# Seven small unread transfers that shift which DMA engines carry the 8-row loads of a sparse-attention and spectral-mixing kernel

## The chip, the cores and the metric

The kernel runs on one core of a Trainium2 chip. The metric is the time of one execution on the device, in microseconds, from the first to the last instruction of that core. Before the change the median of three runs is 434.43 us (434.22, 434.43 and 436.14).

A core has five engines that work side by side, each with its own stream of instructions: TensorE (PE in the profile; its weight loads are PEld), VectorE (DVE), ScalarE (ACT), GpSimd (POOL) and SyncE (SP). Data come from the chip's memory to on-chip memory by 16 DMA engines, which the five engines give work to.

## The reference

The program is an attention with two kinds of sparse masks, followed by a mixing of frequencies and a channel product:

```python
# q, k, v: (8, 8, 576, 64) float32
scores = scale * q @ k^T
mask: heads 0-3: 0 <= i - j < 32          # local
      heads 4-7: j <= i and i % 32 == j % 32   # strided
attn = softmax(scores where mask else -1e9) @ v
x = attn as (8, 576, 512)
X = rfft(x over the 576 positions)             # the first 64 modes are kept
Y[m] = X[m] @ (w_r[m] + 1j * w_i[m])           # 512 x 512 per mode
y = irfft(Y)
u = x + y
out = u + max(u @ w_ch, 0)                     # float32
```

The 64 pairs of matrices w_r and w_i are 134 MB in float32, by far the largest input. Each is used once for 8 batch entries. q, k and v together are 28 MB.

## The kernel before, in words

The batch has 8 entries, called images here. The kernel goes through four stages.

1. Strided heads of all images (the loop around line 746). For each image, 72 rows of 2048 numbers are loaded for each of v, q and k: 4 heads by 18 blocks of 32 positions. They are turned by TensorE, scored, masked, exponentiated and multiplied with v.
2. Local heads of all images (the loop around line 775), with the products of the first half of the modes' weights between them.
3. The second half of the weights (the loop around line 846), with the turning of x and the first parts of the channel product between them.
4. A tail (from line 859) with the last modes, the inverse transform as a matrix product and the output.

The weights are the stream that runs through all of it. `w_fetch` (L174) loads the weights of two modes: one transfer for w_r (L196) and one for w_i, each of 64 rows of 2 x 2048 numbers, which are cast from float32 to float16 on the way. Nearly all loads, those of the weights, of q, k and v, are issued by GpSimd, and therefore stand in one order, the order of the program. The order is written out by hand (`manual_schedule`).

The loads of the strided rows are made by `load_str` (L219). For images 0 and 1 there is one transfer of 64 rows for each tensor and image (L229); later a transfer of 64 rows takes two images at once (L227). The remaining 8 of the 72 rows are always loaded for two images at once, by L231, right behind the 64-row load of the even image. So there are twelve 8-row loads in all: for v, q and k of the image pairs 0/1, 2/3, 4/5 and 6/7. They go into `ring`, a buffer of 12 slots that the local heads' rows (`load_loc`, L233) use later.

The order of the calls matters for the change: `load_str(0)`, `load_str(1)`, `load_str(2)` and one `w_fetch` come ahead of the loop. In the loop, image 1 has `load_str(4)` behind the weights fetched at image 0, and image 3 has `load_str(6)`; behind each come further calls of `w_fetch` and, from image 4 on, the loads of the local rows.

Each transfer that GpSimd issues counts up one of eight semaphores in turn. An issue waits until the transfer eight places before it has landed, and for whatever its buffer needs: that TensorE has read what stood in the slot, for instance.

`pat` (L155) is the pool of buffers that the attention stages use. Its buffers exist once each (bufs=1). A second buffer that is asked for under the same name is the same memory, and whoever writes it waits for the earlier use to end.

Of the kernel before, what the change touches and what calls it, by code (L numbers as in the profile page):

```python
# [11 lines left out]
F16 = mybir.dt.float16  # L12
# [67 lines left out]
def kernel(  # L80
# [10 lines left out]
    nc = tc.nc  # L91
# [63 lines left out]
    pat = actx.enter_context(tc.tile_pool(name="pat", bufs=1))  # L155
# [59 lines left out]
    def loc_in(b, vi):  # L215
        t = ring[:, ds(2 * (b % 6), 2), :].rearrange("p n x -> p (n x)")
        return t[:, ds(1152 * vi, 1152)]

    def load_str(b, nb):  # L219
        for vi in (2, 0, 1):  # L220
            n = 3 * (b % 4) + SLOT[vi]
            two = ring[:, n : n + 4 : 3, :]
            src = SRC[vi][b - b % 2 : b - b % 2 + 2, 4:8].rearrange(
                "b h (c r) d -> (h c) b (r d)", r=32
            )
            if nb == 2:
                nc.gpsimd.dma_start(two[0:64], src[0:64])  # L227
            else:
                nc.gpsimd.dma_start(ring[0:64, n, :], src[0:64, b % 2])  # L229
            if b % 2 == 0:  # L230
                nc.gpsimd.dma_start(two[64:72], src[64:72])  # L231

    def load_loc(*bs):  # L233
        for b in bs:
            if b >= B:
                return
            for vi in (2, 0, 1):
                nc.gpsimd.dma_start(
                    loc_in(b, vi),
                    SRC[vi][b, 0:4].rearrange("h (cb i) d -> (h cb) (i d)", i=18),  # L240
                )
# [455 lines left out]

    psum_pools(tp=3, sc=3, av=2)
    load_str(0, 1)
    const_load(nc.scalar, "cI", "cM6", "cM5", "cFs")  # L700
    load_str(1, 1)
    const_load(nc.sync, "cMl", "cFl", "cA")
    load_str(2, 2)
    w_fetch()

# [269 lines left out]
    for i in range(len(units)):  # L975
        v_rows(i)
        b, t = units[i]
# [42 lines left out]
```

The softmax here doesn't subtract the row's maximum and nothing guards it: scores larger than these inputs give would overflow.

## Time and profile before

| | before |
|---|---|
| time, median of 3 | 434.43 us |
| PE busy | 338.5 us (78%) |
| DVE busy | 215.9 us (50%) |
| ACT busy | 187.5 us (43%) |
| POOL busy | 129.3 us (30%) |
| DMA, chain of work that ended last | 68% of the span |
| weight loads (L196) | 62 + 60 transfers, about 19 us from issue to landing |
| 8-row loads (L231) | 12 transfers, 64 KB written by each, about 12 us from issue to landing |
| weights, last issue of w_i on the chain, then DMA | at 381.88 us, 10.87 us |

How to read the views. The page's second part cuts the span into 40 slices; a digit is a busy share in tenths, and the row GB/s is what the DMA engines moved in the slice, counted as written to on-chip memory. Its third part lists the queues: a queue's name, then its packets, its megabytes, and its share of 16 engines' time. The chain of work that ended last goes back from the last instruction, at each step to what released it; in order of time its lines are start, length, and what ran or was waited for. In the timeline of GpSimd a line is start, length, line, operation, tile and source, and in brackets how long the engine had been idle before and what ended that. A transfer's line on GpSimd is only its issue; the data come later.

### The profile page before, as it was taken

Reading aid. Unit: us, or ns where it says so; the run is one execution under the profiler, and the core shown is the slowest. Engines: PE = TensorE matmul, PEld = TensorE weight load, DVE = VectorE, ACT = ScalarE, POOL = GpSimd, SP = SyncE. Lnnn points to the kernel's source line nnn. Section 1 sums busy time; section 2 is a strip of 40 time slices with the busy share of each in tenths; the row PEclk is TensorE's granted clock in tenths of the full one; section 3 lists DMA queues with packets and bytes.
Section 4 is the critical chain, followed back from the end, with each engine's and each line's share of the span. In section 5 each row is a group of like instructions: output and inputs, shape, how many; then the busy total and the mean of one; then the engine's idle time right before and its main releaser. Section 6 shows DMA issues by size and latency. Waiting matters only on the chain.

```text
span 434.2 us, 12103 instructions
## 1 busy us (share of the span) xinstructions
PE 338.5 (78%) x5307; PEld 244.5 (56%) x5307; DVE 215.9 (50%) x468; ACT 187.5 (43%) x352; POOL 129.3 (30%) x208
## 2 busy tenths in 40 slices
PE   1986888779985787889885566587789798968993
PEld 1865776658864575667753344454456465643441
DVE  2888678744433243342511033355436366503894
ACT  1686678634643435444440401143215123602892
POOL 6433332322332222222222222222222221200992
PEclk9999899865985859875865569887958899988999
DMA  8999999999999999999999999999999999991787
GB/s 176 210 211 213 214 212 213 211 211 213 213 212 212 214 214 212 214 214 213 214 212 213 213 214 214 212 214 215 211 214 214 212 214 214 213 182 30 272 330 261
DMA packets 29140, 92.18 MB, mean 212 GB/s; under 512 B 4064, under 2 KB 5344, under 8 KB 29088
## 3 DMA queue, kind: packets, MB, share of 16 engines
q0 software_dynamic: 24704, 81.28, 94.4%
q1 hardware_dynamic: 3584, 9.59, 5.9%
q8 instruction: 42, 0.69, 0.6%
q10 hardware_dynamic: 800, 0.54, 0.5%
q14 instruction: 10, 0.08, 0.0%
HBM read 163.22 MB, written 9.44 MB: 398 GB/s over the span
## 4 chain that ended last, share of the span: by engine, by line
DMA 68%; PE 19%; DVE 6%; ACT 2%; issue 2%; POOL 1%; DVEq 0%; POOLq 0%
DMA wt<-in_moe_w_i_dram 51%; DMA wt<-in_moe_w_r_dram 11%; DMA ring<-in_q_dram 5%; PE y L547 2%; PE v L689 2%; DVE xb L250 2%; DVE kz L292 2%; PE u L689 2%; PE v L895 2%; PE sc L514 1%; ACT X L260 1%; PE tp L395 1%; DVE rec L249 1%; PE sc L441 1%; PE sc L353 1%
## 5 line engine op out<-in xcount | busy, mean ns | idle before, releaser
L547 PE MATMUL y<-X,wt 128*128 128x16 f16 (+1 forms) x2048 | 82.4, 192 | 61.0 <-DMA wt<-in_moe_w_i_dram 59.4
L547 PEld LDWEIGHTS <-wt 128*128 128x128 f16 (+1 forms) x2048 | 72.9, 103 | 76.5 <-issue 68.5
L196 POOL DMA_DIRECT2D wt<-in_moe_w_r_dram x62 | 36.5, 589 | 141.7 <-PE y L547 67.4
L196 POOL DMA_DIRECT2D wt<-in_moe_w_i_dram x60 | 35.4, 590 | 73.5 <-DMA wt<-in_moe_w_i_dram 61.2
L654 ACT ACTIVATE v<-sc 128x512 f16<-128x512 f32 x32 | 19.1, 597 | 69.7 <-PE sc L645 69.6
L645 PE MATMUL sc<-w_cp,xT 128*128 128x512 f16 (+1 forms) x160 | 48.2, 430 | 0.0
L471 ACT ACTIVATE PL<-sc 128x480 f16<-128x480 f32 (+1 forms) x48 | 27.3, 580 | 46.8 <-PE sc L457 46.5
L655 DVE COPY xo<-tp 128x512 f16<-128x512 f16 x32 | 22.1, 692 | 35.7 <-PE tp L653 35.6
L249 DVE RECIPROCAL rec<-av 90x4 f32<-90x4 f32 (+2 forms) x80 | 14.7, 184 | 46.2 <-PE av L486 34.8
L250 DVE TENSOR_TENSOR xb<-av,rec 90x256 f16<-90x256 f32 (+2 forms) x80 | 36.0, 450 | 2.7
L402 DVE COPY qT<-tp 128x576 f16<-128x576 f16 x16 | 12.0, 758 | 38.8 <-PE tp L395 35.9
L260 ACT ACTIVATE v<-tp 128x640 f16<-128x640 f16 (+1 forms) x24 | 19.4, 808 | 24.9 <-PE tp L429 22.1
L395 PE MATMUL tp<-cI_s,ring 64*64 64x64 f16 x864 | 26.7, 213 | 0.8 <-DVE qT L402 0.6
L360 ACT ACTIVATE PL<-sc 90x360 f16<-90x360 f32 (+1 forms) x48 | 22.7, 491 | 6.1 <-PE sc L353 5.3
L929 DVE TENSOR_TENSOR osb<-u,rl 128x512 f32<-128x512 f32 (+1 forms) x37 | 23.7, 674 | 1.8 <-PE u L689 1.1
L395 PEld LDWEIGHTS <-ring 64*64 64x64 f16 x864 | 21.1, 125 | 5.7 <-issue 2.6
L910 POOL TENSOR_TENSOR rl<-rl,xo 128x512 f32<-128x512 f32 x16 | 18.3, 1157 | 18.2 <-ACT rl L908 17.9
L441 PE MATMUL sc<-cMl_s,cI_s 128*128 128x480 f16 (+1 forms) x48 | 22.5, 468 | 1.6 <-ACT X L260 1.6
L457 PE MATMUL sc<-qT,kz 128*128 128x160 f16 (+1 forms) x160 | 22.4, 267 | 0.0
L908 ACT ACTIVATE rl<-v 128x512 f32<-128x512 f32 x36 | 20.4, 600 | 4.7 <-PE v L689 3.9
L285 PE MATMUL tp<-cI_s,ring 72*128 72x72 f16 x256 | 15.1, 206 | 9.4 <-DMA ring<-in_v_dram 7.9
L260 ACT ACTIVATE kz<-tp 64x360 f16<-64x360 f16 (+1 forms) x32 | 19.1, 595 | 7.7 <-PE tp L395 6.1
(103 smaller groups left out, 655.7 us busy)
## 6 DMA issues: line engine op xcount, KB each, us to landing
wt<-in_moe_w_r_dram POOLq DMA_DIRECT2D x62, 512.0 KB, 19.0
wt<-in_moe_w_i_dram POOLq DMA_DIRECT2D x60, 512.0 KB, 19.4
out_dram<-osb SPq DMA_DIRECT2D x14, 512.0 KB, 2.7
ring<-in_v_dram POOLq DMA_DIRECT2D x8, 288.0 KB, 13.3
ring<-in_q_dram POOLq DMA_DIRECT2D x8, 288.0 KB, 13.6
ring<-in_k_dram POOLq DMA_DIRECT2D x8, 288.0 KB, 13.5
ring<-in_v_dram POOLq DMA_DIRECT2D x3, 512.0 KB, 15.0
ring<-in_q_dram POOLq DMA_DIRECT2D x3, 512.0 KB, 14.8
```

Source lines behind the costliest of these rows:

```text
L196: nc.gpsimd.dma_start(dst, rows)
L250: nc.vector.tensor_tensor(out=dst, in0=val.rearrange("p h (q c) -> p h c q", c=4), in1=rec[0:n, 0:pieces] .to_broadcast((n, pieces, 64)) . ...
L260: nc.scalar.activation(out=out, in_=in_, func=ACTF.Copy)
L360: nc.scalar.activation(out=PS[0:n, ds(POFF[t], 4 * n)], in_=scp[0:n, 0 : 4 * n], func=ACTF.Exp, scale=SCALE,)
L395: nc.tensor.transpose(tp[ds(64 * hp, 64), ds(64 * i, 64)], qn[ds(64 * hp, 64), ds(64 * (9 * g + i), 64)], idn[ds(64 * hp, 64), ds(64 * hp, ...
L441: nc.tensor.matmul(scp[:, 0 : n * times].rearrange("p (h x) -> p h x", h=times), idn, mask_rows("cMl", n, times), start=True, stop=False,)
L457: nc.tensor.matmul(scp[:, ds(col, n)], kzs[par][:, hp, ds(s0, 128)], qTs[par][:, ds(s0, n)], start=False, stop=(i == len(todo) - 1),)
L471: nc.scalar.activation(out=dst, in_=src, func=ACTF.Exp, scale=SCALE)
L547: nc.tensor.matmul(yv[:, mi, e, :], wt[pr, XC[c], ds(128 * e, 128)], Xh[half][pr, c, :, :, m], start=(c == 0), stop=(c == 3),)
L645: nc.tensor.matmul(vp[pr, :], xT[:, ch, cols], w_chs["cp"][:, ch, :], start=(ch == 0), stop=(ch == 3),)
L655: nc.vector.tensor_copy(out=xo[pr].rearrange("p (h q c) -> p h q c", h=2, c=4), in_=tp[pr, 0:512].rearrange("p (h c q) -> p h q c", h=2, c=4),
L929: nc.vector.tensor_tensor(out=osb[:, t % 2, cols], in0=up[:, cols], in1=rls[b, t][:, t % 2, cols], op=AluOp.add,)
```

## The change

`lower_engines` issues a small transfer: the first 8 rows of w_ch, of each two pieces of 8 numbers (32 bytes), into a buffer named `step` that nothing reads. It is called ahead of each 8-row load. It issues the transfer only if the number of 8-row transfers so far, its own counted too, is odd, and not ahead of the k loads of the image pairs 0/1 and 2/3. Seven such transfers are added.

They are there for the DMA engines: an 8-row transfer occupies eight of the 16, and the next 8-row transfer the other eight. The extra transfers take a turn each, so that ten of the twelve 8-row loads go to the same eight engines and two to the other eight.

```diff
+    eights = []
+
+    def lower_engines(no):
+        if len(eights) % 2 and not no:
+            t = pat.tile([8, 2, 16], F16, name="step")
+            src = moe_w_ch[0:8].rearrange("p (a x) -> p a x", a=2)
+            nc.gpsimd.dma_start(t[:, :, 0:8], src[:, :, 0:8])
+            eights.append(0)
+
     def load_str(b, nb):
         for vi in (2, 0, 1):
             n = 3 * (b % 4) + SLOT[vi]
@@ -228,7 +237,9 @@
             else:
                 nc.gpsimd.dma_start(ring[0:64, n, :], src[0:64, b % 2])
             if b % 2 == 0:
+                lower_engines(b < 4 and vi == 1)
                 nc.gpsimd.dma_start(two[64:72], src[64:72])
+                eights.append(1)
```

## The prediction

> **What bounds the kernel now.** I read the page's slices first, then the queues and the chain of work that ended last.
>
> ```profile
> DMA  8999999999999999999999999999999999991787
> GB/s 176 210 211 213 214 212 213 211 211 213 213 212 212 214 214 212 214 214 213 214 212 213 213 214 214 212 214 215 211 214 214 212 214 214 213 182 30 272 330 261
> ...
> q0 software_dynamic: 24704, 81.28, 94.4%
> ...
> q8 instruction: 42, 0.69, 0.6%
> ...
> DMA 68%; PE 19%; DVE 6%; ACT 2%; issue 2%; POOL 1%; DVEq 0%; POOLq 0%
> ```
>
> For 36 of 40 slices the 16 DMA engines are full, at a flat 210 to 215 GB/s, and 68% of the chain is DMA. The chain in order of time says which transfers end last:
>
> ```profile
> 28.19 14.84 DMA ring<-in_q_dram
> 43.08 0.66 PE tp L269 x8
> ...
> 362.00 19.60 DMA wt<-in_moe_w_r_dram
> 381.60 0.28 issue
> 381.88 10.87 DMA wt<-in_moe_w_i_dram
> 392.88 0.64 PE y L547 x16
> ```
>
> From 105.9 us the chain hangs on the weights and leaves them only at 392.88; the 41.5 us of tail behind that aren't touched. So the change is worth what it does to the landing of the last weights. A transfer lands when the slowest of the 16 engines has done its part, so I read single engines. The trace holds every packet's start, and of every transfer 16 marks, one for each engine's part. The last weight load's marks, in us: 387.49, .78, .79, 388.11, .12, .13, .74, 389.23; then 392.81, .91, .92, .94, .96, 393.44, .56, .94. Eight engines are some 4.9 us ahead of the other eight. At 25.1 to 26.8 us (first weights) there was no such gap.
>
> The gap is the instruction queue's: 42 fetches of 16,384 B, each with its packet 0.89 to 0.97 us long from the third on, and the eight lengths repeat in turn (893, 893, 948, 945, 935, 974, 974, 961 ns): eight engines take turns. A fetched engine's own next packet comes 0.88 to 0.94 us after the fetch began, and its later marks stay about 1.06 us late. By the last weights each of the eight has had five: 5.3 us, less what idling early took up; 4.9 is seen.
>
> **Which eight.** Call A the engines of the first 8-row load, B the others. I followed packets through the 8-row loads of images 4 and 6: an engine with a share runs two packets of 4096 B 305 ns apart and its mark (0.63 us); an engine without one runs three small packets (about 0.04 us); the roles swap with each load, six loads for each half. A fetch starts within 1 ns of when one engine's next packet was due. The engines fetched at 27.68, 56.35 and 65.32 us are of B. At 35.67, 46.67 and 74.59 us near-equal packets let either half fit. I take it that B is the fetched, late half, at about 4 in 5.
>
> **What the Trainium skill says.** "DMA: Bandwidth & Descriptors", section "Why a DMA increments its semaphore by 16 and not by 1": a transfer of GpSimd whose outer size gives fewer than 16 parts goes to that many consecutive engines from a cursor that moves round, and all 16 engines post. The trace agrees: alternating halves, 16 marks. The section "Queues, rings and completion order" says that each engine consumes its ring in order; the packets agree (the small packets of an engine without a share come behind its earlier weights, not at once). So a small transfer's last mark waits for everything queued before it.
>
> **The change part by part.** (1) Seven steps, L225, each move the cursor by eight. The order becomes: image 0: A, step, A, B; image 2: A, step, A, B; image 4: A, step, A, step, A; image 6: step, A, step, A, step, A. A gets ten loads, B two; steps fall on B. Four loads change side, each 0.63 − 0.04 = 0.59 us for an engine: A +2.36 us, B −2.36.
>
> (2) The steps' own time: on A three small packets each, 7 × 0.04 = 0.3 us. On B two reads of 32 B and a mark each; not in the trace; between 0.04 us (as A) and 0.63 us (a true share); I take 0.06, so 0.4 us. Pool: 7 issues at 0.57 us (row L231 of this view) = 4 us, hidden: Pool waits for landings there.
>
> ```profile
> 28.19 0.57 POOL L231 DMA_DIRECT2D ring<-in_q_dram  x1 [0.24 <-DMA wt<-in_moe_w_i_dram]
> 30.97 0.58 POOL L227 DMA_DIRECT2D ring<-in_k_dram  x1 [2.21 <-PE sc L353]
> 32.91 0.57 POOL L231 DMA_DIRECT2D ring<-in_k_dram  x1 [1.35 <-DMA wt<-in_moe_w_i_dram]
> 35.32 0.58 POOL L196 DMA_DIRECT2D wt<-in_moe_w_r_dram  x1 [1.84 <-DMA wt<-in_moe_w_r_dram]
> ```
>
> The waits here are of one kind: eight transfers may be open, so each issue waits for the one eight before it. Issues run some 12 us ahead of landings.
>
> (3) New waits. All steps write one buffer (bufs=1, one name), so in the built order each step also waits until the step before has landed. For image 4's k step that is the step three transfers back; also for image 6's q and k steps. (Image 6's v step waits for one seven back: about the old rule.) Behind the waiting step on Pool are all later loads. So Pool stands still for about the 10 to 12 us that a transfer now takes from issue to landing, and when it goes on only two transfers are left in the engines' queues, an 8-row load and a 64-row load, instead of seven.
>
> What happens at the last of these, with x the packet time of the awaited mark on the slowest engine. A mark is seen about 0.35 us after its packet; Pool starts 0.28 us after a mark (5.70 to 5.99, 7.80 to 8.08, 9.72 to 10.00). So Pool issues the step at x + 0.63, the 8-row k load at x + 1.21, the first weights at x + 1.78. From issue to first packet: the very first load shows 1.64 us (1.24 to 2.88). The weights can start at x + 3.42. An A engine has until then 0.63 + 2.46 (64-row load, eight packets) + 0.63 = 3.72 us of work: it doesn't run dry. A B engine has 2.46 us, less its lead: it stands idle, and starts the weights at x + 3.42, only 0.3 us ahead of A. The lead that four loads gave it is gone; the same at the stall in image 4, and in part at the next.
>
> (4) Sum. A reaches the weights behind image 6 at 4 × 0.59 + 0.3 = 2.65 us later than now. Before, the halves are level there (six loads each, last 8-row load's marks 62.04 to 63.98), so B comes 2.65 − 0.3 = 2.35 us later. From there on B takes its fetches as before. Engines already fetched once are levelled, but the two whose first fetch is at 74.6 and 81.4 us have all five ahead and keep the full delay: last mark 393.94 + 2.35 = 396.3. A ends at 389.23 + 2.65 = 391.9, before B, so it doesn't set the end. Time: 434.43 + 2.35 = **436.8 us**.
>
> The attention stage slips too: image 6's q lands now at 61.06 and is used at 61.66, and would land about 2 us later. The weights slip as much, so that adds nothing. If B isn't the fetched half, the late engines in A carry +2.65 and the result is the same.
>
> The unknown: issue to first packet. At 1.0 us (the issue's own 0.57 and little else) B keeps 0.95 us: +1.7, 436.1. At 2.4 us A idles 0.5 us too: +3.1, 437.5.
>
> **Rivals.** (a) Balance: the stalls cost B nothing, since the queue holds enough. A ends at 391.9, B at 393.94 − 2.36 + 0.4 = 392.0. Gain 1.95: **432.5 us**, not slower. For: the gap of 4.9 us is just twice 2.36. Against: only two transfers stay queued at three places. (b) Part of the lead survives, say half of the 4.7 us between the halves: **434.5 us**. For: the awaited marks may come sooner when fetched B engines, not A, are last. (c) Starvation: A too runs dry at each of the three stalls, by 0.5 us each, 1.5 us on top of the forecast: **438.3 us**. For: 3.72 against 3.42 us is a thin margin, three times. Against: every issue of the stretch shown takes 0.57 or 0.58 us, so the burst itself has little spread.
>
> **How the numbers follow.** Forecast 0.52, (a) 0.22, (b) 0.12, (c) 0.14. The bound of 0.5% is at 432.26 and 436.60. The forecast's own spread, 436.1 to 437.5, lies about two thirds above: 0.35; with (c) slower is 0.49. Of (a) about half may pass 432.26: faster 0.12. The rest, 0.39, is within. Range: 432.5 to 438.2 leaves out the faster half of (a), 0.11, and half of (c), 0.07: under 2 in 10.
>
> **What would show it.** Right: on Pool three waits of the step (L225) for a landed step, the two in images 4 and 6 that stand behind a full queue near 10 us; behind them a burst of issues 0.6 us apart; slices of DMA share with a dip near 44 and 62 us; the last weights' issue to landing about as now, but PE's first product after them near 395.2 instead of 392.88; marks still in two groups. Wrong: marks of the last weights within 2 us of each other and PE starting near 391 (balance); or the waits gone because the steps land before they are asked for.

## The result, and the profile after

| | before | after |
|---|---|---|
| time, median (6 runs each, same chip) | 434.44 us (434.13 to 436.14) | 439.98 us (439.03 to 442.18) |
| ratio | | 1.0127, interval 1.0103 to 1.0150 |

The change makes the kernel 5.5 us slower; 2.35 us were forecast, and the range ended at 438.2. The page's row GB/s after (40 slices of some 10.9 us), and its chain by line:

```profile
GB/s 172 210 212 205 175 167 200 212 212 210 214 212 214 215 212 215 212 214 214 213 212 214 214 213 215 214 212 214 213 214 213 214 213 213 214 210 43 265 336 265
...
DMA wt<-in_moe_w_i_dram 49%; DMA wt<-in_moe_w_r_dram 12%; DMA step<-in_moe_w_ch_dram 7%; PE y L558 3%; PE sc L656 2%; DMA ring<-in_q_dram 2%; PE v L700 2%; PE u L700 2%; DMA ring<-in_v_dram 2%; PE v L906 2%; PE tp L406 1%; DVE xb L261 1%; PE sc L525 1%; DVE kz L303 1%; POOL wt L196 1%
```

Before, the row GB/s was flat from the second slice on. Now slices 4 to 7 (some 33 to 77 us) read 205, 175, 167, 200; the others ahead of the tail are as before. A transfer that writes 256 bytes, the step, has 7% of the chain. The chain in order of time, its two steps and its end:

```profile
28.32 14.91 DMA step<-in_moe_w_ch_dram
43.23 0.28 issue
43.51 0.56 POOL step L225
...
47.48 13.95 DMA step<-in_moe_w_ch_dram
61.43 0.28 issue
61.71 0.49 POOL step L225
62.26 3.10 DMA ring<-in_q_dram
...
386.92 10.88 DMA wt<-in_moe_w_i_dram
397.94 0.64 PE y L558 x16
```

The last weights take the same 10.88 us from issue to landing, but PE gets them at 397.94 instead of 392.88: 5.06 us later. GpSimd's timeline shows the waits (idle time in brackets):

```profile
43.51 0.56 POOL L225 DMA_DIRECT2D step<-in_moe_w_ch_dram  x1 [9.53 <-DMA step<-in_moe_w_ch_dram]
44.06 0.55 POOL L241 DMA_DIRECT2D ring<-in_k_dram  x1
44.61 0.60 POOL L196 DMA_DIRECT2D wt<-in_moe_w_r_dram  x1
...
61.71 0.56 POOL L225 DMA_DIRECT2D step<-in_moe_w_ch_dram  x1 [12.44 <-DMA step<-in_moe_w_ch_dram]
62.26 0.56 POOL L241 DMA_DIRECT2D ring<-in_q_dram  x1
...
64.42 0.56 POOL L225 DMA_DIRECT2D step<-in_moe_w_ch_dram  x1 [1.00 <-DMA step<-in_moe_w_ch_dram]
```

Two waits of some 10 us and one of 1.00. What they do to the DMA engines is seen when the same stretches are cut into single microseconds (last columns: granted PE clock, mean DMA share, GB/s). Before:

```profile
44.00:45.00 1.00, 1.00 (x11) 0.96 (x9) 0.24 (x1) 0.47 (x1) 0.10 (x1) 0.50 1.06 209
...
62.00:63.00 1.00, 1.00 (x18) 0.94 (x15) 0.58 (x2) 0.47 (x1) 0.33 (x1) 1.00 1.04 205
```

After:

```profile
43.00:44.00 1.00, 0.50 (x13) 0.38 (x11) 0.92 (x4) 0.80 (x2) 0.49 (x1) 1.00 0.68 135
44.00:45.00 1.00, 0.16 (x6) 0.06 (x3) 1.00 (x3) 0.47 (x1) 1.00 (x3) 1.00 0.46 86
45.00:46.00 1.00, 1.00 (x19) 0.94 (x19) 0.85 (x2) 0.20 (x1) 1.00 (x3) 1.00 0.51 66
...
62.00:63.00 1.00, 1.00 (x14) 0.79 (x12) 0.61 (x1) 0.33 (x1) 1.00 (x3) 0.50 0.20 37
63.00:64.00 1.00, 0.81 (x13) 0.64 (x10) 0.41 (x2) 0.75 (x3) 0.42 (x1) 0.50 0.35 33
64.00:65.00 1.00, 0.00 (x0) 0.00 (x0) 0.18 (x1) 0.38 (x1) 0.58 (x2) 0.50 1.00 152
```

Before, every microsecond of these stretches moved 205 GB/s or more. Now nearly all 16 engines stand idle twice, not one half of them. A measure of it is the mean of a transfer's 16 marks, in us (in brackets its lead or lag against before):

| mean of the marks of | before | after |
|---|---|---|
| image 4's k, 64 rows (last load ahead of the first stall) | 44.34 | 44.57 (+0.2) |
| the first weights behind it | 47.22 | 49.73 (+2.5) |
| image 6's k, 64 rows | 62.65 | 67.87 (+5.2) |
| the first weights behind it | 65.42 | 70.98 (+5.6) |
| the last weights | 390.68 | 396.13 (+5.4) |

Almost all is lost by 71 us, some 2.3 us at the first stall and 2.9 at the second, and from there to the end the lag stays between 5.4 and 5.9 us. For the last weights the last mark lags by 5.0 us, no more than the mean: in this kernel no unevenness between the engines is left over from ten loads on one half. The last marks still stand in two groups, 393.43 to 394.55 and 397.67 to 398.99.

The two spans (434.2 and 437.4) differ by only 3.2 us, because the profile of before is one of its longer runs: there PE had a granted clock of 0.50 from 394.7 to 398.1 us, just behind the last weights (the same four products took 1.71 us and here 0.99, at 1.00), and the tail took 41.3 us instead of 39.5.

```profile
395.50 1.71 PE y L887 x4
```

```profile
400.19 0.99 PE y L898 x4
```

### The profile page after: what moved, and what is told of

Read it like the earlier page. It is cut to its first block, busy times and chain, and to the rows that moved or that the text cites. A ratio compares the mean times of both kernels' runs of the same rounds, so it can differ in the third digit from the quotient of the medians.

```text
span 437.4 us, 12114 instructions
## 1 busy us (share of the span) xinstructions
PE 342.6 (78%) x5307; PEld 246.1 (56%) x5307; DVE 216.2 (49%) x468; ACT 187.8 (43%) x352; POOL 132.9 (30%) x215
## 4 chain that ended last, share of the span: by engine, by line
DMA 71%; PE 18%; DVE 3%; issue 3%; POOL 1%; ACT 1%; DVEq 0%; POOLq 0%
DMA wt<-in_moe_w_i_dram 49%; DMA wt<-in_moe_w_r_dram 12%; DMA step<-in_moe_w_ch_dram 7%; PE y L558 3%; PE sc L656 2%; DMA ring<-in_q_dram 2%; PE v L700 2%; PE u L700 2%; DMA ring<-in_v_dram 2%; PE v L906 2%; PE tp L406 1%; DVE xb L261 1%; PE sc L525 1%; DVE kz L303 1%; POOL wt L196 1%
## 5 line engine op out<-in xcount | busy, mean ns | idle before, releaser
L656 PE MATMUL sc<-w_cp,xT 128*128 128x512 f16 (+1 forms) x160 | 51.3, 452 | 0.0
L656 PEld LDWEIGHTS <-xT 128*128 128x128 f16 (+1 forms) x160 | 14.8, 111 | 13.9 <-issue 6.9
```

Of the source, the lines that this page charges most:

```text
L656: nc.tensor.matmul(vp[pr, :], xT[:, ch, cols], w_chs["cp"][:, ch, :], start=(ch == 0), stop=(ch == 3),)
```

## The experiments

The change does two things at once: it moves loads to other engines, and it adds waits through the one buffer. The first four runs separate them. A step of 16 rows has a part for each engine and leaves the place where it is; a buffer of its own for each step takes its wait away.

**Own buffers: the new places without the waits.**

```diff
-            t = pat.tile([8, 2, 16], F16, name="step")
+            t = pat.tile([8, 2, 16], F16, name=f"step{len(eights)}")
```

> Each of the seven steps writes a buffer of its own, so none waits for the step before; the loads' places stay ten to A and two to B. Theory W (the loss is the steps' wait for each other, which empties the engines' queues): the dips of the DMA rate near 44 and 63 us are gone, and with them the whole loss; if B is the fetched half the balance shows, 432 to 433 us, if not 436 to 437. Rival P (the loss comes from the steps themselves, their issues, their places among the eight open transfers, their small packets): 439 to 440 us as with the shared buffer.

**16 rows in one buffer: the waits without the new places.**

```diff
-            t = pat.tile([8, 2, 16], F16, name="step")
-            src = moe_w_ch[0:8].rearrange("p (a x) -> p a x", a=2)
+            t = pat.tile([16, 2, 16], F16, name="step")
+            src = moe_w_ch[0:16].rearrange("p (a x) -> p a x", a=2)
```

> The steps have 16 rows instead of 8, so that all 16 engines take a share and the cursor comes back to where it was: the 8-row loads alternate as in the kernel before, six to each half. The one shared buffer and its waits stay. W: the dips stay, and most of the loss, 438 to 440 us. Rival Q (the loss comes from ten loads on one half, the wrong one): 434 to 435 us.

**16 rows, own buffers: neither.** Both edits together, so the rows are 16 and each step has a buffer of its own.

> Steps of 16 rows, each with its own buffer: neither the waits nor the new places, only seven more transfers. W: within 0.2% of the kernel before, 434 to 435 us. Rival P: 439 to 440 us.

**The other half.** Own buffers, and one step more ahead of the first 8-row load, so that ten loads go to half B.

```diff
             if b % 2 == 0:
+                if b == 0 and vi == 2:
+                    t = pat.tile([8, 2, 16], F16, name="first")
+                    ...
+                    nc.gpsimd.dma_start(t[:, :, 0:8], src8[:, :, 0:8])
```

> As the first of these four (own buffers), with one more step ahead of the first 8-row load, so that ten loads go to the other eight engines. If the fetched engines are those of B: these carry 4 x 0.59 us more, 436.5 to 437 us, and the last weights' two groups of marks lie near 9 us apart. If they are those of A: 432 to 433 us. If four are in each half: 436 to 437 us both here and in the first.

Measured on one chip, against 435.03 us for the kernel before:

| | time, us | ratio, interval |
|---|---|---|
| own buffers, ten on A | 440.47 | 1.0128 (1.0115 to 1.0141) |
| 16 rows, one buffer | 441.03 | 1.0131 (1.0115 to 1.0147) |
| 16 rows, own buffers | 435.06 | 1.0009 (0.9997 to 1.0020) |
| own buffers, ten on B | 437.42 | 1.0057 (1.0045 to 1.0069) |

Steps of 16 rows in buffers of their own cost nothing, and they leave the loads where they were: at image 6's k the last of the 16 marks lags by 1.7 us against before and their mean by 1.4, a lag that stood at 25 us already; with ten on A it is 4.0 against 1.8. The waits alone cost 6.0 us, as much as the whole change. The new places alone cost 5.4 us on A, and 2.4 on B. That is harmful on either side: what I expected of the first run, that the loss goes when the waits go, failed, the balance that the rival (a) hoped for isn't there, and my reading of "which eight" can't be right as it stood. And the two don't add up: 6.0 and 5.4 alone, 5.5 together. The slices of the run with 16 rows in one buffer look like those of the changed kernel, those with own buffers of 16 rows like before from the third on:

```profile
GB/s 167 202 210 213 158 161 195 211 212 210 214 211 215 214 213 213 214 212 214 214 212 213 214 214 213 215 212 214 214 213 214 213 213 213 213 204 38 271 331 258
```

```profile
GB/s 166 197 209 213 212 211 212 210 212 212 213 213 214 212 215 213 213 214 213 213 212 213 214 212 215 213 213 215 212 214 213 214 213 213 213 185 29 273 329 266
```

**Do the waits wipe out the places?** The changed kernel, its one buffer kept, with the step "first" of the run above, so that ten loads go to B.

> The changed kernel, its shared buffer kept, with one more step (in a buffer of its own) ahead of the first 8-row load, so that ten loads go to the other half. With buffers of their own the two halves differed by 3 us (440.5 with ten on A, 437.4 with ten on the other). Theory D (the waits drain all engines at 44 and at 62 us, which levels them, so that where the loads before fell no longer counts): 439.5 to 441, the same as the changed kernel. Theory S (waits and places both count and would add): 3 us under the changed kernel, 436.5 to 437.5.

**One stall of the two.** 16-row steps in one buffer, but own buffers for image 6's three, so that only image 4's k step waits. The edit, against the run with 16 rows in one buffer:

```diff
-            t = pat.tile([16, 2, 16], F16, name="step")
+            t = pat.tile([16, 2, 16], F16, name=f"step{len(eights) if len(eights) > 12 else 0}")
```

> The 16-row steps (no load changes its engines), with the one shared buffer for the steps of images 0, 2 and 4, and a buffer of its own for each of image 6's three. Only the stall of image 4 is left: its k step waits for its q step. Both stalls together cost 6 us (441.0). Theory D (each stall costs what all 16 engines stand idle in it: in the changed kernel the mean of the marks slips by 2.3 us at the first and 2.7 at the second): 436.8 to 437.6, one dip near 45 us and none near 63. Theory L (only the slowest engine's delay counts, 0.6 to 1.7 us at the first stall, the rest at the second): 435.2 to 436.3.

Measured, against 434.93 us: with ten on B and one buffer 441.79 (1.0169, interval 1.0131 to 1.0206), with one stall 438.66 (1.0081, 1.0054 to 1.0108). So with the waits in place it brings nothing to put the ten loads on the half where they had cost 3 us less: the time isn't under that of the changed kernel (ratio 1.0127, 1.0103 to 1.0150), it is if anything above. That speaks for the waits levelling the engines, and against a sum. One stall alone costs 3.7 us, above the 1.9 to 2.7 that I had written, but not under: what one stall costs is not the slowest engine's 0.6 to 1.7 us. On the mean of the marks this trace is 0.6 us behind ahead of the stall, 2.4 at the first weights behind it, and 2.9 from 88 us on. It has the one dip and not the other:

```profile
44.00:45.00 1.00, 1.00 (x19) 0.94 (x20) 0.46 (x1) 0.18 (x1) 0.99 (x3) 1.00 0.42 78
45.00:46.00 1.00, 1.00 (x15) 1.00 (x13) 0.00 (x0) 0.46 (x2) 1.00 (x3) 0.77 0.58 70
...
62.00:63.00 1.00, 0.61 (x14) 0.48 (x12) 0.91 (x3) 0.96 (x3) 0.77 (x2) 0.80 1.06 201
63.00:64.00 1.00, 0.00 (x0) 0.00 (x0) 0.11 (x1) 0.30 (x1) 0.00 (x0) 0.50 1.12 225
```

**More work behind the awaited transfer.** If a wait costs only what the engines run out of, it must become free once enough is queued behind it, though Pool waits as before.

```diff
         for vi in (2, 0, 1):
+            if (b, vi) in ((4, 1), (6, 0), (6, 1)):
+                w_fetch()
...
-        w_fetch([2, 1, 1, 1, 1, 1, 0, 0][b])
+        w_fetch([2, 0, 1, 0, 0, 1, 0, 0][b])
```

> The 16-row steps with the one shared buffer (441.0: both stalls, no load moved to other engines), and three pairs of weight loads, which came behind the loads of images 4 and 6, issued among them instead: one pair ahead of image 4's k, one ahead of image 6's q, one ahead of its k. All waits of the steps stay as they are, three transfers back becomes five, but each now has 4.9 us more of work queued behind the transfer that it waits for. Theory D (a wait costs just what the engines run out of work in it, 1 to 3.5 us each so far): no dips near 45 and 63 us, 434.5 to 436.5, and within 1 us of the next run. Theory T (the wait costs by the time that Pool stands still, whatever is queued): 440 to 442.

> The kernel before with the same three pairs of weight loads issued among the loads of images 4 and 6, and no steps: the control for the run with waits. The DMA engines' work is the same and the rows come in some 5 us later at images 4 and 6. Both theories: 434 to 436; more only if attention, now fed later, holds the loads back.

Measured, against 434.76 us: with the waits 437.94 (1.0073, 1.0049 to 1.0097), the control without steps 435.77 (1.0027, 1.0011 to 1.0043). The timeline of the run with waits still shows four of them (idle time in brackets), and the single microseconds show no dip beside them:

```profile
43.06 0.50 POOL L225 DMA_DIRECT2D step<-in_moe_w_ch_dram  x1 [4.31 <-DMA step<-in_moe_w_ch_dram]
51.44 0.51 POOL L225 DMA_DIRECT2D step<-in_moe_w_ch_dram  x1 [5.55 <-DMA step<-in_moe_w_ch_dram]
...
66.57 0.51 POOL L225 DMA_DIRECT2D step<-in_moe_w_ch_dram  x1 [4.95 <-DMA step<-in_moe_w_ch_dram]
```

```profile
44.00:45.00 1.00, 1.00 (x18) 1.00 (x15) 0.27 (x1) 0.47 (x1) 1.00 (x3) 1.00 1.06 213
...
62.00:63.00 1.00, 0.96 (x22) 0.74 (x18) 0.92 (x4) 0.89 (x3) 0.00 (x0) 1.00 1.04 209
```

19 us of standing still on Pool (the one left out is 4.51 us), and both stalls are gone. By 103 us, where this trace has the same loads behind it as the kernel before, the mean of the marks is only 0.1 us later than there, and in the changed kernel 5.5 us: up to here the waits cost nothing. The moved weights are missed elsewhere: the eleventh slice (about 109 to 120 us) reads 154 GB/s in this run and 169 in the control, and between the loads that before land near 112.6 and 115.1 us the lag of the mean jumps from 0.2 to 3.2 us, in the control from 0.7 to 2.8. It stays at that. The time is 1.4 us over what I expected, and the 2.2 us between the two medians aren't accounted for: in the two traces the last weights land within 0.6 us of each other (the control's trace is of one of its longer runs, 437.93 us). So this run shows where the stalls' cost comes from; whether the waits add to the later gap it doesn't show.

**Why new places cost, without any wait.** The next three runs ask. First a weighing of the halves: four more 8-row loads of full size, one at a time between weight loads (they land between 185 and 239 us), where all queues are full, each followed by a step so that all four go to A; and the same shifted by four engines. The loads are extra and nothing reads them. The part that calls them:

```diff
...
+            if i in (46, 52, 58, 64):
+                late_load()
+                late_step(8)
```

> The kernel before with four more 8-row loads of the true size (image 0's q rows again, into a part of the ring that nothing reads any more), one at a time between weight loads in the second quarter of the run, each followed by an 8-row step of 16 bytes a row, so that all four shares fall on half A (the engines of the first 8-row load) and none on B. Nothing else changes, and every load around them is a large one. What is weighed is which engines end last: 4 x 0.63 = 2.5 us of extra work for each A engine. Theory M (the eight engines that are fetched from lie in both halves): 437.2 to 437.8, and of the eight late marks of the last weight load only some move up by 2.5 us. Theory FA (A is the fetched half): 437.2 to 437.8, and all eight late marks move up. Theory FB (B is the fetched half, as the prediction had it): 434.9 to 435.4, and only the eight early marks move up.

> As the run with late pairs on A, but a 4-row step ahead of the first pair moves the place by four engines, so that the four shares fall on the upper four engines of A and the lower four of B (a 12-row step moves it back afterwards). If the fetched engines are a block of eight neighbours, the count of late marks that move by 2.5 us differs from that with A, and it tells where the block begins: none moved means 434.9 to 435.4, and then this place is where extra work costs nothing. If they lie spread (every second engine or so), about four of eight move again, as with A, and the time is again 437.2 to 437.8.

**Two 16-row steps at each place,** own buffers: no waits, no new places, only more small transfers.

```diff
             nc.gpsimd.dma_start(t[:, :, 0:8], src[:, :, 0:8])
+            t = pat.tile([16, 2, 16], F16, name=f"more{len(eights)}")
+            nc.gpsimd.dma_start(t[:, :, 0:8], src[:, :, 0:8])
```

> The 16-row steps with buffers of their own (which cost nothing), but two at each of the seven places: still no load changes its engines and no step waits for another. Only the number of small transfers among the eight that may be open goes up, in images 4 and 6 from six of each nine to twelve of fifteen or so. Theory W (small transfers take up places among the eight open ones, so the engines hold less work and run dry, wherever the loads fall): 437 to 440, with dips in the DMA share near 45 to 65 us and Pool waiting 2 us ahead of each small issue. Theory I (what costs in the run with own buffers and ten loads on one half is the imbalance alone): 434.9 to 436, and no dips.

Measured, against 434.64 us: pairs on A 436.93 (1.0043, 1.0024 to 1.0061), shifted 437.81 (1.0076, 1.0049 to 1.0102), two steps at each place 437.58 (1.0073, 1.0050 to 1.0097). The last weights' eight late marks, in us:

```text
before            392.81 392.91 392.92 392.94 392.96 393.44 393.56 393.94
late pairs on A   393.49 393.62 394.10 394.15 394.17 394.77 395.75 396.13
shifted by four   393.37 393.82 394.29 395.53 395.57 395.96 396.27 397.12
```

With the pairs on A (a run whose marks were 0.4 us late already at 120 us) two of the eight stand out; shifted, five or six do. The extra loads' own marks agree: from the weights ahead of the third one on A to that load, two of the eight late marks move by 0.9 us, and six only by 0.16 to 0.19, so these are engines without a share of it. So the late engines lie in both halves, more of them in B, and no half is free of them. The weighing wasn't quite clean: in the shifted run slice 23 (some 239 to 250 us) reads 195 GB/s, where the engines that were ahead ran out (eight of a weight load's marks lie within 0.35 us there). The run with ten loads on B fits: six of its late marks lie at 396.02 to 396.77, two at 393.5. That is the first part of the cost of new places: whichever half gets ten, it holds some of the engines that end last.

The second part is in the run of doubled steps. It moves no load to other engines, no step waits for another, and it loses 2.9 us, in dips:

```profile
44.00:45.00 1.00, 1.00 (x14) 0.85 (x13) 0.45 (x1) 0.00 (x0) 1.00 (x2) 0.50 1.02 140
...
61.00:62.00 1.00, 0.86 (x18) 0.68 (x19) 0.95 (x4) 0.93 (x2) 0.72 (x2) 1.00 0.84 111
```

Eight transfers may be open, large or small, and each issue waits for the slowest engine's mark of the one eight before: at 51.85 and 54.33 us Pool issues the two steps after waits of 1.96 and 1.98 us, each for a landing of weights. The more of the eight are small, the less work the engines hold, and the engines that are ahead run out first. Single steps leave enough while the engines are about level (no dip with 16 rows and own buffers). With ten loads on A they aren't: there the first weights behind image 6 have marks from 66.9 to 71.0 us (64.5 to 66.4 before), and the dips come back, without a single wait for a step:

```profile
62.00:63.00 1.00, 1.00 (x25) 0.91 (x25) 0.88 (x2) 0.43 (x2) 1.00 (x3) 1.00 0.83 160
63.00:64.00 1.00, 0.14 (x5) 0.01 (x1) 0.60 (x2) 0.84 (x3) 0.29 (x1) 1.00 0.95 164
```

The marks say how the two parts share the cost. With ten on A and own buffers their mean lags by 0.9 us at 25 us (1.3 with 16 rows and own buffers, where it then grows by no more than 0.3), by 1.8 at image 6's k, by 2.5 at the first weights behind it and by 3.8 to 4.5 from 88 us to the last weights but one. The last mark of a load lags there by another 1.6 us (median over the loads). So most of the loss is time in which the engines as a whole moved less, and the smaller part is that the late engines are later than the mean. With ten on B the mean lags by 2.1 to 2.3 us from 65 us on, and the last mark by another 1.0.

**An attempt at a faster kernel.** It cuts four weight loads into 8 + 8 + 48 rows at a quiet place, and puts both 8-row pieces on what I took for the eight early engines. The part that cuts them:

```diff
...
+                    if i in (44, 50, 56, 62) and not ri:
+                        nc.gpsimd.dma_start(dst[0:8], rows[0:8])
+                        late_step(8)
+                        nc.gpsimd.dma_start(dst[8:16], rows[8:16])
+                        late_step(8)
+                        nc.gpsimd.dma_start(dst[16:64], rows[16:64])
+                        continue
```

> The kernel before, with nothing in the attention loads changed. From the late pairs I read that the fetched engines are places 6 to 13, counted from the first engine of half A (two of A's eight moved up, six of the shifted eight). So places 14, 15 and 0 to 5 have the lead of 4.9 us. Four weight loads of 64 rows, in the second quarter, are cut into 8 + 8 + 48 rows, with an 8-row step of 16 bytes a row (each in its own buffer) behind both 8-row pieces, after a 14-row step has moved the place by 14: both pieces go to places 14 to 5, which then have 5 rows where they had 4, the fetched ones 3. That moves 4 x 0.6 = 2.4 us of work from the late engines to the early ones. Theory N (the block is read rightly, and a balance helps where the queues stay full): 432.2 to 433.2, and the last load's marks within some 2 us of each other. Theory O (the fetched engines are elsewhere): 434.5 to 437.5, and the late marks split. Theory R (small transfers among large ones make engines run dry even here): 435 or more, with dips in the DMA share between 150 and 230 us.

Measured: 438.75 us (1.0083, 1.0058 to 1.0108). Slices 21 to 23 read 200, 169 and 208 GB/s: four small transfers at a time empty the engines here too (theory R), which hides whether the balance helps. Two late marks stand apart at 397.25 and 397.41, so the block doesn't seem to have been read rightly either; whether a 14-row step moves the place by 14 I didn't test by itself. No kernel of these beats the one before.

## Why the prediction was wrong

Point by point:

- **What bounds it, and that only the landing of the last weights counts:** right. They come 5.06 us later, the time is 5.54 us longer. That the tail isn't touched holds for its work; its length varies from run to run by some 2 us with the PE clock.
- **(1) Ten loads on A cost or gain ±2.36 us:** without meaning in the changed kernel. The stalls level the engines after most of the loads: the 16 marks of the first weights behind image 4 lie 1.2 us apart, before 2.6. Waits without moved loads take 441.03 us (ratio 1.0131), ten on A with waits 439.98 (1.0127), ten on B with waits 441.79 (1.0169), and the intervals overlap.
- **Which eight:** the assumption that B is the fetched half fell; the late engines lie in both. It did no harm to the number, since nothing of the places survived, but rival (a) got its 22% from it.
- **(2) The steps' own time, and Pool's 4 us hidden:** right as far as it was run, 435.06 against 435.03 us with 16-row steps in own buffers; 8-row steps weren't run without their move.
- **(3) The waits:** the waits came as forecast: waits of 9.53 and 12.44 us, Pool going on 0.28 us after the mark, bursts 0.55 to 0.6 us apart, dips at 44 and 62 us. The sentence on order that the prediction takes from "Queues, rings and completion order" stands there in the paragraph on the queues of SyncE and ScalarE; that GpSimd's queue keeps its order on each engine is what this case shows: the step's 16 marks, 40.40 to 43.23 us, come 0.16 to 0.21 us behind those of the 64-row load ahead of it.
- **The failed step** is the size in (3), "An A engine has until then 0.63 + 2.46 (64-row load, eight packets) + 0.63 = 3.72 us of work: it doesn't run dry", from which I let each stall cost no more than B's lead, and that once (+2.35). Three things in it were off. The stall that I worked out, the last, is the one that cost nothing visible (a wait of 1.00 us); the two before it cost 2.3 and 2.9 us, each anew, because a lead that is gone after the first comes back by the second: the 16 marks of the weights at 55.51 us lie 1.2 us apart, those of the next, at 58.83, 2.0 us. Then, the 3.72 us are counted from the awaited mark on the *slowest* engine. At the second stall ten engines had made that mark by 59.74 us, fifteen by 60.70, and one only at 61.43, so the others were in part through the work queued behind the mark when Pool was let go. Packets in flight fell from 17 at 61.25 us to none at 63.25. And the packets behind an idle stretch took longer: see the end.
- **Issue to first packet, 1.64 us:** for the 8-row load it was 1.27 us at both stalls (44.06 to 45.33, 62.26 to 63.53), for the 64-row load behind the second 1.40 (62.81 to 64.21), under the value that I took and within its bounds. "DMA: Bandwidth & Descriptors", section "Latency and other measured facts", in the Trainium skill has about 1 us to the first byte for GpSimd's transfers; measured from the start of the issue this trace agrees roughly.
- **(4) The sum:** "B comes 2.35 us later"; all 16 marks came later, those of the last weights, taken in order, by 4.9 to 6.0 us. That the marks stay in two groups, and the last weights' time from issue to landing, were right (10.88 us).
- **Rival (c), starvation,** was the one that happened. I gave it 0.14 and 0.5 us a stall, on the ground that a margin of 0.3 us was thin; it was no margin for the engines ahead. That the change is slower was forecast with the right part of the chain, the waits, but the size came from the lead of one half, and no such lead set it.

What stays open: why ten loads on A go on losing until 88 us, and ten on B not after 65 us; why ten on B with waits is slower than ten on A, if it is; and what the 2.2 us between the run with work behind the waits and its control are.

## What to carry to other kernels

A wait on the engine that issues all transfers is priced by the work queued *behind the awaited transfer*, counted on the engine that is farthest ahead, not on the slowest; count it for each wait by itself, because queues fill and drain again between two. If that work is less than the wait's way back (here 2.8 us, from the last mark at 61.43 to the first packet of the next 64-row load at 64.21), engines stand idle, and here nothing later repaid it. Where the number of open transfers is limited, a tiny one takes the place of a large one, so even transfers that cost no time by themselves, in buffers of their own, can empty the engines: one 16-row step at each place did not (435.06 us), two did (437.58).

## What the runs showed of the hardware

- Packets of 4096 B took 322 to 324 ns in a full stream (112 packets at 42 to 44.2 us before). Behind the second stall the first ones of the eight engines with the 8-row load took 558 to 708 ns (63.53 to 63.61 us after), the first ones of the other eight 386 to 944 ns (64.22 to 64.39), and single later ones up to 1381; behind the first stall it was up to 1564 ns. So at 64 to 65 us the engines are busy (share 1.00) at 152 GB/s: here a drained queue cost more than its idle time. Why the packets took longer no run shows.
- The eight lengths of the instruction fetches, 0.89 to 0.97 us, come in the same order before and after, with single longer ones (1098 ns at 81.01 us after). After the first stall, when the engines were level, the fetch at 56.79 us goes with one late engine: the last mark of the next three transfers stands 0.7 to 0.9 us behind the second last, down to the 61.43 us that the step waited for. That the fetch made it late is inferred from the times.
